# S4D convolution and feed-forward block on one core: the first part's tasks in another order, and evictions shared out anew

## The chip, the cores and the metric

One core of a Trainium2 chip runs the whole program. The metric is the device time of one execution in microseconds; the time before is the median of three runs. A profile of one execution gives every instruction's start and length on the five engines: PE (matmuls; PEld is its weight load), DVE (VectorE), ACT (ScalarE), POOL (GpSimd) and SP, which issues the DMAs.

## The reference

Sequence length 2048, width 640, state size 128, inner width 1728, all float32. `A` is the state-space convolution, `B` the feed-forward part:

```python
def A(u, ...):                      # S4D, by a transform of length 4096
    dt = exp(log_dt)
    A = -exp(log_A_real) + 1j * A_imag
    C = (C_real + 1j * C_imag) * dt[:, None]
    P = exp((A * dt[:, None])[:, :, None] * arange(L))
    K = 2.0 * einsum("dn,dnl->dl", C, P).real
    y = irfft(rfft(u_t, 2 * L) * rfft(K, 2 * L))[:, :, :L]
    return y + u * D_skip

def B(x, w1, w3, w2):
    return (silu(x @ w1) * (x @ w3)) @ w2

mod = silu(c) @ w_mod               # six rows: sa, ca, ga, sb, cb, gb
h = layernorm(x) * (1 + ca) + sa
x = x + ga * A(h)
h = layernorm(x) * (1 + cb) + sb
x = x + gb * B(h)
```

## The kernel before

The program has two parts. The first computes `x + ga * A(h)` up to the inverse transform, the second is the second layernorm and the feed-forward part, written as ordinary code; the change does not reach it.

The first part is a plan of 1507 small tasks. The width of 640 is cut into five blocks b = 0 to 4 of 128 columns, and each block goes through the same steps. A task's name says which: `g2.7` is the eighth chunk (16 columns) of block 2. The tasks that the prediction speaks of are:

- `al8b`, `expb`, `magb`: the table of exponents of block b (a product of 128x1024 by POOL or DVE, the exponentials by ACT, a product of 128x512 by POOL or DVE); `tb.h.0` to `.5` are its tables of phases.
- `gb.c.ph`, `.z0` to `.z2` (POOL, phases `ph` and sizes `xx`, `yy`), `.s0` to `.s4` (ACT, sines `tr`), `.m0` to `.m4` (DVE, products `xx`, `yy`), `.p` (PE, the chunk's kernel rows `kps`, in one half of a PSUM bank), `.r` (ACT, copied to `ks`).
- `hb.i.l`, `.n`, `.x`, `.a`, `.o`: a quarter of the block's normalised input is loaded (`xq`; for block 0 into `sp`), normalised (`hn`, four instructions on DVE or ACT), multiplied, added to (`hb`, DVE), and stored to DRAM (`hs`); `hb.f` fetches it back transposed (`xb`).
- `hhb.i.m` and `kb.i.m`: the first transform of the input and of the kernel (PE, `ps<-wk,xb` and `ps<-wk,ks`), with the evictions `.e` to `sp`, which are a COPY on DVE or an ACTIVATE on ACT.
- `wb.i.f` and `.k`: the second transform (PE, `fh` and `fk`), `.h` the eviction of `fh` to `hq` (ACT), `.x0`, `.x1`, `.c` the complex product (DVE `fp`, `fk`; POOL for w4.2 and w4.5), and `zb.j.z` the first step back (PE, `fz`), with evictions `.v0`, `.v1` to `zt` on DVE or ACT and stores to `zd` in DRAM.
- `hscale` and `fold` (DVE): the scale of the normalisation from the statistics of `xs`, and the rows of `mod` folded in. `fs0` (POOL, `wl`, `w2l`) splits feed-forward weights ahead of time.

What sets the order is the string `ORDER` (from L35 on), a list of all tasks by number, written out. `Plan.run` goes through it, and where a task may run on two engines the letter behind the number (a ACT, d DVE, p POOL) chooses one. The wrapper `InOrder` (L147) chains each instruction to the one written before it on the same engine, so that every engine, SP's DMA issues included, works through its tasks in the order of the list and waits in place for whatever is not ready:

```python
for x in ORDER.split():
    n, (engs, f, after) = T[int(x.rstrip("adp"))]
    ...
        f(dict(a="ACT", d="DVE", p="POOL")[x[-1]] if len(engs) > 1 else engs[0])
```

All instructions of the first part therefore show the wrapper's line, L147, in the profile. Fetches from DRAM are paced: such a DMA waits for the PE instruction written last before it. The product `.p` takes the halves of its bank in turn, in the order in which the products stand in the list.

Of the kernel before, what the change touches and what calls it, by code (L numbers as in the profile page):

```python
# [34 lines left out]
1 2 8 7 12 78 80 3 79 86 81 41 14 19 82 20 42 84 21 15 83 43 85 16 153p 44 17 4 22 154 18 23 28 61 45 59 30 120 31 46 121 24  # L35
10 29 25 39 156 35 26 13 62 157 60 158 47 72 74 70 76 66 89 27 48 5 93 87 91 98 49 36 100 33 95 50 94 34 51 32 88 37 52 38
155p 40 92 159d 53 96 160 90 9 161 6 54 102 162 170 104 55 173 99 11 174 171 97 56 103 186 179 175 57 105 181 176 172 58 190
187 111 180 107 188 67 195 101 122 189 68 191 177 196 163 197 192 64 182 178 123 193 183 109 164 166d 65 184 194 202 113 313
114 115 110 199 185 112 298 117 203 335 206 118 204 124 303 138 308 140 167 198 211 116 212 108 106 168 205 165 142 127 207
336a 208 209 213 119 214 130 131 210 218 63 128 132 139 129 134 215 141 216 143 200 69 419p 71 222 223 133 135 169 422 425p  # L40
423 219 221 234 220 426 235 237 236 125 136 304d 229 420 224 309a 310 305 227 144 75 73 77 126 311 228 217 314a 201 225 226
306 146 339 427 421p 250 424 230 231 315 232 251 252 253 312 299a 238 307 300 316 244 301 317 302 243 239 245 340a 240 233 241
242 254 246 255 256 337 145 247 259 248 147 341 257 261 260 258 338d 148d 262 266 270 267 268 269 282 318 149 150 263 275 151
271 249 272 342a 264 273 265 277 276 343 428 278 152 283 285 284 274 345 286 279 327 280 333 329 436 0 564 569 344a 287 288
289 291 346d 293 292 294 328a 290 281 440 334a 441 330a 442 437 439 438 452 570d 445 295 571 447 572 446 319 565a 137 579 566
443 448 320a 456 444 325 296 457 321 322a 331 453 454 567 326d 461 462 347 332d 449 458 297 323 349 348a 459 324a 460 568 829
573 580d 351 450 357 350d 581 429 684p 685 430 455 468 484 432p 469 470 471 582 830d 353 352 463 831 464 465 832 354 834 583
574 358 835a 472 575a 836 355 356 837 477 576 1359 577 466 368 359 408 370 473 474 369 409 475 1360a 451 360 479 361 478 362
371 480 476 488 467 489 487 433 434 431 686p 485 486 435 500 687 949p 578 839 833 584 481 1361 494 372 493 373 495 1362 374
391 482 490 491 392 492 840a 375 503 516 501 502 1109 838 585 1363 586 1099 376 1110a 504 385 497 496 841 377 498 842 378 1111  # L50
379 509 1112 510 843 587 380 402 505 511 506 507 483 386 499 508 520 383a 512 513 514 598 521 381a 403 522 599a 523 515 590
591a 517 518 519 532 1100d 526 525 1101 527 1102 588 536 524 528 589d 384 844 1113 363 602 537 845a 364a 535 533 688 534 548
689 529 543 366d 541 530 387 551 549 846 542 847 388 690d 691 692 550 538 603a 539 596 540 597a 552 389 545 390 544 557 558
592 593a 600 594 1103 1364 382 365 848 1104 849 404 1365a 546 1366 850 851 1094 367 852 405 601a 595a 553 554 693 406 559 407
# [1842 lines left out]
```

## Time and profile before

| | |
|---|---|
| median of 3 runs | 945.79 us (944.59 to 947.17) |
| the profiled execution's own time | 945.84 us |
| its span | 944.0 us |
| busy in the span | PE 849.6, DVE 700.5, ACT 515.1, POOL 346.4 us |
| first matmul of the feed-forward part | 374.6 us |

The span is what the profile covers; the profiled execution's own time is 1.8 us longer. The busy shares are means over two parts that differ: in the first 374.6 us all engines work, in the rest PE works nearly alone. Waits are named by what ended them; "issue" is a wait that nothing in the profile explains.

### The profile page before, as it was taken

What the parts mean: (1) busy time and instruction counts of PE and PEld (TensorE: products, weight loads), DVE (VectorE), ACT (ScalarE), POOL (GpSimd) and SP (SyncE); (2) the same over time, 40 slices, a digit from 0 to 9 for tenths busy, and PEclk for the clock granted to TensorE, in tenths of its full rate; (3) what the DMA queues carried; (4) which work ended last, traced back from release to release, by engine and by line L of the source; (5) the groups of instructions that cost most, each with busy time, mean ns of one, the idle gap of its engine ahead of it and who ended that gap; (6) DMA issues with size and microseconds to landing.
All of it is one profiled execution on the core that took longest, in us unless ns stands there. A gap on an engine that the chain in (4) does not pass through costs nothing.

```text
span 944.0 us, 22044 instructions
## 1 busy us (share of the span) xinstructions
PE 849.6 (90%) x8963; PEld 674.2 (71%) x8963; DVE 700.5 (74%) x1232; ACT 515.1 (55%) x886; POOL 346.4 (37%) x355
## 2 busy tenths in 40 slices
PE   2176779899999887999999999999999999999997
PEld 1035768767868653777877788888888888888775
DVE  7898999999999856476666666376567777765663
ACT  5889999899888733333333244354343444454331
POOL 2799999899989552000000000001133333100000
PEclk9587989999999998999999999999999999999999
DMA  9985556133041658965525262322132211123242
GB/s 244 241 255 126 170 147 170 48 104 103 27 124 40 177 149 232 254 182 153 151 64 146 84 161 77 111 84 70 42 84 70 57 50 48 38 77 111 77 149 82
DMA packets 124941, 112.78 MB, mean 119 GB/s; under 512 B 12328, under 2 KB 107048, under 8 KB 123560
## 3 DMA queue, kind: packets, MB, share of 16 engines
q1 hardware_dynamic: 124072, 110.46, 43.0%
q8 instruction: 70, 1.15, 0.5%
q10 hardware_dynamic: 768, 0.92, 0.4%
q14 instruction: 31, 0.25, 0.1%
HBM read 90.38 MB, written 20.97 MB: 118 GB/s over the span
## 4 chain that ended last, share of the span: by engine, by line
PE 67%; DMA 10%; DVE 8%; ACT 6%; issue 3%; POOL 3%; SPq 1%; DVEq 0%; ACTq 0%; POOLq 0%
PE p L820 17%; PE acc L1067 16%; PE gu L1030 6%; PE gu L1032 6%; PE gu L1031 6%; PE ps L147 4%; PE fz L147 3%; DMA low<-zd 3%; PE kps L147 2%; PE fk L147 2%; DVE yy L147 2%; PE fh L147 2%; DVE fp L147 1%; DMA wq<-in_w 1%; ACT hn L147 1%
## 5 line engine op out<-in xcount | busy, mean ns | idle before, releaser
L1030 PE MATMUL gu<-xh,wh 128*128 128x512 f32 x270 | 106.2, 398 | 1.9 <-ACT xh L609 1.1
L1032 PE MATMUL gu<-xh,wl 128*128 128x512 f32 x270 | 105.4, 390 | 0.0
L1031 PE MATMUL gu<-xl,wh 128*128 128x512 f32 x270 | 105.2, 390 | 0.0
L147 ACT ACTIVATE tr<-ph 128x512 f32<-128x512 f32 (+1 forms) x160 | 92.9, 599 | 7.0 <-DVE yy L147 5.5
L839 POOL TENSOR_TENSOR ws<-wp 128x256 f32<-128x256 f32 x13 | 9.6, 739 | 230.9 <-DVE x L610 116.0
L147 POOL TENSOR_TENSOR ph<-p,p 128x1024 int32<-128x1024 int32 x40 | 78.2, 1955 | 3.0 <-ACT tr L147 2.7
L147 DVE TENSOR_TENSOR yy<-yy,tr 128x512 f32<-128x512 f32 (+1 forms) x80 | 75.4, 942 | 1.5 <-ACT tr L147 1.2
L723 ACT ACTIVATE wh<-wr 128x640 fp32r<-128x640 f32 x51 | 34.9, 731 | 70.5 <-PE gu L1031 55.6
L820 PE MATMUL p<-x,wch 128*128 128x512 f32 x208 | 68.3, 389 | 0.0
L1030 PEld LDWEIGHTS gu<-xh,wh 128*128 128x128 f32 x270 | 50.6, 188 | 18.3 <-issue 2.1
L147 PE MATMUL kps<-yy,xx 128*32 128x64 f32 x2560 | 49.3, 228 | 10.8 <-DVE xx L147 4.6
L1032 PEld LDWEIGHTS gu<-xh,wl 128*128 128x128 f32 x270 | 50.7, 188 | 11.2 <-DVE wl L733 0.4
L736 POOL MEMSET w2l<- 64x640 f32 x1 | 0.6, 631 | 157.8 <-PE acc L1067 157.8
L1031 PEld LDWEIGHTS gu<-xl,wh 128*128 128x128 f32 x270 | 50.7, 188 | 10.2 <-DVE xl L610 0.2
L147 DVE TENSOR_TENSOR xx<-tr,xx 128x512 f32<-128x512 f32 x80 | 54.3, 680 | 1.1 <-ACT tr L147 0.8
L857 DVE TENSOR_TENSOR s<-p,s 128x512 f32<-128x512 f32 x52 | 34.7, 682 | 27.0 <-ACT s L855 23.0
L147 POOL TENSOR_TENSOR yy<-e,e 128x512 f32<-128x512 f32 x48 | 52.7, 1109 | 4.5 <-PE kps L147 2.5
L147 PEld LDWEIGHTS kps<-yy,xx 128*32 128x32 f32 x2560 | 43.2, 113 | 11.6 <-POOL yy L147 4.5
L1045 DVE TENSOR_TENSOR a<-a,gu 128x512 f32<-128x512 f32 x26 | 17.8, 686 | 45.0 <-PE gu L1032 44.9
L1043 ACT ACTIVATE th<-gu 128x512 f32<-128x512 f32 x26 | 15.5, 596 | 64.3 <-PE gu L1032 64.3
L147 PE MATMUL ps<-wk,xb 128*64 128x128 f32 x640 | 47.1, 296 | 3.0 <-ACT sp L147 1.4
L147 PE MATMUL fh<-sp,wb 128*64 128x128 f32 x640 | 44.4, 284 | 4.9 <-DVE fp L147 2.2
(377 smaller groups left out, 2380.8 us busy)
## 6 DMA issues: line engine op xcount, KB each, us to landing
wr<-in_w SPq DMA_DIRECT2D x52, 320.0 KB, 3.7
zd<-zt SPq DMA_DIRECT2D x39, 256.0 KB, 2.7
w2r<-in_w SPq DMA_DIRECT2D x26, 320.0 KB, 3.1
wp<-in_w SPq DMA_DIRECT2D x26, 320.0 KB, 3.6
wq<-in_w SPq DMA_DIRECT2D x26, 320.0 KB, 3.2
low<-zd SPq DMA_DIRECT2D x48, 160.0 KB, 5.8
xs<-in_x SPq DMA_DIRECT2D x16, 320.0 KB, 10.3
hs<-hb SPq DMA_DIRECT2D x20, 256.0 KB, 2.4
```

Of the source, the lines that this page charges most:

```text
L147: self.prev = self.k.order(f(*a, **kw), self.prev)
L723: self.nc.scalar.activation(wh[:, i], raw[:, i], AF.Copy)
L736: self.nc.gpsimd.memset(w2l[64:].bitcast(F32), 0.0)
L820: nc.tensor.matmul(to, t[:, o], y[:, k], start=start and k == i == 0, stop=stop and (k, i) == (n - 1, 2), skip_group_check=True)
L839: G.tensor_tensor(s[0], a21, a22, op=ALU.add)
L857: add = lambda o, bk, s: V.tensor_tensor(o, bk, s, op=ALU.add)
L1030: nc.tensor.matmul(pg, wh[:, k, :], xh[:, k, :], start=(k == 0), stop=False)
L1031: nc.tensor.matmul(pg, wh[:, k, :], xl[:, k, :], start=False, stop=False)
L1032: nc.tensor.matmul(pg, wl[:, k, :], xh[:, k, :], start=False, stop=(k == KT - 1))
L1043: nc.scalar.activation(th, gu[0], AF.Tanh, scale=0.5)
L1045: nc.vector.tensor_mul(a, a, gu[1])
L1067: nc.tensor.matmul(acc[k], *two(a, w), start=(m == 0 and i == 0), stop=(m == 12 and i == 2))
```

## The change

Only the string `ORDER` differs. It has the same 1507 numbers in another order, and for some tasks another letter. It is one line shorter, so that the wrapper's line is L146 afterwards. The first line of it stands for the rest:

```diff
 ORDER = """
 
-1 2 8 7 12 78 80 3 79 86 81 41 14 19 82 20 42 84 21 15 83 43 85 16 153p 44 17 4 22 154 18 23 28 61 45 59 30 120 31 46 121 24
+1 2 3 4 78 79 5 80 6 81 20 14 82 19 7 41 84 8 21 83 15 11 42 153d 9 43 154 22 44 23 16 24 17 25 18 45 30 59 26 28 27 96 91 87 29
 ...
 """
```

Engines: 25 evictions go from DVE to ACT and 17 from ACT to DVE; of the normalisations `.n` four go to ACT and three to DVE; al80, al81, mag0, mag1 and four table steps go from POOL to DVE, two table steps from DVE to POOL.

At the start, SP issued `w_mod` (into `sp`) and two tables ahead of the loads of x (`xs`), here from the last parameter load on:

```order
L147 DMA x_e<-in_a_im 128x5x128
L147 DMA sp<-in_w_mod 128x1920 x2
L147 DMA wk<-in_t_wk 128x256
L147 DMA wz<-in_t_wz 128x256
L147 DMA xs_164<-in_x 32x2560 x2
L147 DMA xs_164<-in_x 32x4x640 x2
L147 DMA xs_194<-in_x 32x2560 x2
L147 DMA xs_194<-in_x 32x4x640 x2
L147 DMA sp<-in_w_mod 128x1920
```

Now all four loads of x stand directly behind the parameters:

```order
L146 DMA x_e<-in_a_im 128x5x128
L146 DMA xs_142<-in_x 32x2560 x2
L146 DMA xs_142<-in_x 32x4x640 x2
L146 DMA xs_147<-in_x 32x2560 x2
L146 DMA xs_147<-in_x 32x4x640 x2
L146 DMA xs_170<-in_x 32x2560 x2
L146 DMA xs_170<-in_x 32x4x640 x2
L146 DMA xs_176<-in_x 32x2560 x2
L146 DMA xs_176<-in_x 32x4x640 x2
L146 DMA sp<-in_w_mod 128x1920 x2
```

The loads of x moved ahead of all of `w_mod`; the two tables follow later. POOL's first products before (the row with `al` is al80, that with `mag` mag0, the first `ph` is the phase of chunk g0.0):

```order
L147 TENSOR_TENSOR ks_133<-al,j_109 128x1024
L147 TENSOR_TENSOR x_e<-x_e,pB 128x128
L147 TENSOR_TENSOR p_118<-p_118,step 128x128x2
L147 TENSOR_TENSOR p_118<-p_118,step 128x128x4
L147 TENSOR_TENSOR x_e<-x_e,pB 128x512
L147 TENSOR_TENSOR pB<-pB,x_e 128x128
L147 TENSOR_TENSOR e_122<-e_122,mag 128x128x4
L147 TENSOR_TENSOR p_119<-p_119 128x128
L147 TENSOR_TENSOR p_119<-p_119,step 128x128x2
L147 TENSOR_TENSOR ph_312<-p_118,p_119 128x1024
```

And now:

```order
L146 TENSOR_TENSOR x_e<-x_e,pB 128x128
L146 TENSOR_TENSOR p_118<-p_118,step 128x128x2
L146 TENSOR_TENSOR pB<-pB,x_e 128x128
L146 TENSOR_TENSOR p_118<-p_118,step 128x128x4
L146 TENSOR_TENSOR x_e<-x_e,pB 128x512
L146 TENSOR_TENSOR p_119<-p_119 128x128
L146 TENSOR_TENSOR p_119<-p_119,step 128x128x2
L146 TENSOR_TENSOR ph_298<-p_118,p_119 128x1024
```

The two products with `al` and `mag` are gone from POOL's list; DVE has them. On PE the place that matters is the product of chunk g2.7 (`kps` from `yy_368`; `yy_352` is chunk g2.6; `fh26` is w2.6's, `fk17` w1.7's). Before:

```order
L147 MATMUL fk17_3107<-sp_85,wb_84 64x128 x8
L147 MATMUL kps_391<-dsk_74,ident_58 32x4 x4
L147 MATMUL kps_391<-yy_352_3001,xx_352_3000 32x64 x32
L147 MATMUL fh26_3160<-sp_85,wb_84 64x128 x8
L147 MATMUL fh27_3169<-sp_85,wb_84 64x128 x8
L147 MATMUL fh25_3178<-sp_85,wb_84 64x128 x8
...
L147 MATMUL ps306_3257<-wk_72,xb_86 64x4x16x2 x8
L147 MATMUL ps304_3266<-wk_72,xb_86 64x4x16x2 x8
L147 MATMUL kps_391<-dsk_74,ident_58 32x4 x4
L147 MATMUL kps_391<-yy_368_3007,xx_368_3006 32x64 x32
```

The "..." stands for k2.0's 32 rows. Now the same place reads:

```order
L146 MATMUL kps_427<-yy_352_2766,xx_352_2765 32x64 x32
L146 MATMUL fz110_3037<-fp12_2741,wz_73 128x512
L146 MATMUL fz111_3038<-fp12_2741,wz_73 128x512
...
L146 MATMUL fk14_3053<-sp_85,wb_84 64x128 x8
L146 MATMUL fk16_3074<-sp_85,wb_84 64x128 x8
L146 MATMUL kps_427<-dsk_74,ident_58 32x4 x4
L146 MATMUL kps_427<-yy_368_2857,xx_368_2856 32x64 x32
L146 MATMUL fh21_3132<-sp_85,wb_84 64x128 x8
L146 MATMUL fh23_3144<-sp_85,wb_84 64x128 x8
L146 MATMUL fk15_3160<-sp_85,wb_84 64x128 x8
L146 MATMUL fk17_3172<-sp_85,wb_84 64x128 x8
```

The product of g2.7 moved up past the `fh` of block 2, k2.0 and two input transforms of block 3 (`ps306`, `ps304`), which now come behind it. Near the end of the first part w4.0's and w4.1's `fk` come ahead of w4.2's, six evictions of block 4 go to ACT, and `fs0`, which POOL did between two steps of w4.2, is last. The products `gb.c.p` now run in the order of their numbers (g0.0, g0.1, g0.2 ...), where before some pairs were swapped (g0.0, g0.2, g0.1 ...), so that a chunk's rows may lie in the other half of their bank.

More of the change, by code (lines that the diff above doesn't have):

```diff
@@ L39 @@
[L39 to L54, printed above, removed]
@@ new lines @@
+562 712 707 1369 389 639 695 623 711 708 718 1106 650 721 713 640 720 563 850 393 709 1103 1107 719 365 722 714 1108 633 651
+697d 727 733 723 667 390 547 724 728 616 668 726 949p 725 394 715 737 730 634 729 617 698 851 610 734 738 395 731 736 612d 396
+950 673 735 742 611d 749 852 1095d 607 696 739 608d 1096 656 752 674 743 1097 699 744 604 740 750 700 609d 741 745 865 751 606a
+605a 746 853 716 765 753 866d 754 759 747 854a 760 755 952 758 414 657 1370d 769 756 867 766 415a 761 417a 757 768 613 418 1371
@@ new lines @@
+1073 1163 1221 926 1082 1079 1147 1074 1152 1164 1081 919 910 1083 1080 1075 1084 920 1222 1153 1087 934 1045 1219 1089 1085
+913a 1088 940 911a 935 1223 1231 1086 912 1076 936 941 927 1091 1235 1247 1090 1061 937 928a 1482 1092 1248 914 1236 942 929
+930a 1140 943 1232 1237 1137 1216d 1077 1093 1141a 1142d 1234 1238 1380 1197 1139a 1233 1242 1186 1138d 1239 1250 1241 1134 1187
+1240 1249 1198 1251 1243 1381 944 1224 1136a 1135d 1252 1244 1253 1143 1257 945a 1263 1258 1245 947a 1144d 1145a 1256 1254 1382
@@ new lines @@
+1165 1267 1264 1259 1255 1203 1266 1260 1268 1148 1166 1269 1279 1167 1169 1246 1149 1204 1274 1483 1180 1225 1283 948 1168
+1227p 1261 1181 1150 1265 1270 1272 1170 1391 1228 1273 1282 1271 1275 1395 1280 1151 1284 1397 1281 1396a 1276 1285 1290 1171
+1226 1288 1286 1393 1289 1229 1287 1291 1392a 1277 1230 1295 1172 1154 1398d 1173 1389 1299 1296 1174 1300 1297 1155 1394a 1487
+1387 931 1301 1390d 946 1311 1292 1383 1262 1278 1156 1293 1305 1384a 1298 1302 1304 1175 1294 1307 1312 1315 1388a 1157 1314
@@ new lines @@
+1316 1306 1176a 1488 1158 1313 1178a 1320 1177 1303 1179 1322 1317 1327 1321 1199 1308 1161a 1318 1205 1200 1319 1323 1182 1343
+1159a 1201 1331 1484 1385 1206 1160 1183 1309 1386a 1207 1332 1202 1188 1328 1324 1208 1330 1489 1325 1347 1184 1336 1470 1344
+1189 1435 1471 1185 1345 1333 1338 1428 1346 1353 1436 1190 1310 1492 1209 1329 1348 1162 1191 1349 1337 1429 1352 1411 1334
+1210d 1212a 1485 1402 1335 1211 1412 1340 1404a 1493 1192 1354 1350 1339 1403a 1326 1399 1195a 1351 1196 1341 1356 1193a 1401a
@@ L88 @@
+1355 1194 1405 1213 1357 1406a 1417 1358 1407a 1400a 1464 1418 1342 1497 1481 1408 1452 1410a 1409a 1490 1486 1413 1419 1414
+1453 1420 1498 1465 1430 1421 1437 1415 1431 1432 1416 1446 1422 1433 1438 1499 1423 1439 1434 1440 1426a 1494 1454 1447 1448
+1455 1424a 1449 1500 1441 1450 1456 1425 1427 1495 1457 1466 1442d 1451 1502 1467 1458 1472 1443 1468 1444a 1473 1496 1445 1459
+1469 1474 1475 1460a 1503 1476 1462a 1461 1463 1491 1501 1477a 1479a 1478 1480 1504 1505 1506
 """
```

67 lines of the change are left out of this document (31 added, 36 removed).

## The prediction

> **What bounds the kernel now.** I read first the busy time of each engine, cut into five stretches at points of the program (the end of the input statistics, the last vector product of chunk g2.7, the last spectrum product on TensorE, the first matmul of the feed-forward part), then what the engines wait for in the second and third of them. The columns of the windows are time, length, then busy microseconds and instruction counts of PE, PEld, DVE, ACT and POOL, granted clock, DMA share and rate.
>
> ```profile
> core 0: us, PE busy (x) PEld busy (x) DVE busy (x) ACT busy (x) POOL busy (x), PEclk, DMA share, GB/s
> 0.00:67.50 67.50, 24.29 (x253) 12.06 (x257) 57.87 (x123) 47.31 (x99) 43.11 (x61) 0.77 0.93 242
> 67.50:228.40 160.90, 133.40 (x3096) 110.89 (x3088) 154.96 (x264) 149.74 (x269) 150.77 (x146) 0.94 0.49 133
> 228.40:335.10 106.70, 100.17 (x2748) 81.67 (x2750) 96.42 (x159) 85.13 (x155) 85.64 (x80) 1.00 0.32 86
> 335.10:374.60 39.50, 31.50 (x239) 17.20 (x233) 26.17 (x76) 11.81 (x20) 15.91 (x14) 0.91 0.76 206
> 374.60:944.00 569.40, 560.22 (x2638) 452.41 (x2638) 365.11 (x614) 221.15 (x347) 51.01 (x57) 1.00 0.37 102
> ```
>
> The feed-forward part, 569.4 us, is PE almost alone (560.2 busy), and its code and order are the same in both kernels, so only the first 374.6 us can change. There the bound changes hands. From 67.5 to 228.4 DVE is busy 154.96 of 160.90 us (96%) while PE has 27.5 us without work; from 228.4 to 335.1 PE is busy 100.17 of 106.70 (94%). The hand-over is one place in the order, the product g2.7.p:
>
> ```profile
> 225.90 0.68 DVE L147 TENSOR_TENSOR xx<-tr,xx 128x512 f32<-128x512 f32 x1
> 226.50 1.20 DVE L147 TENSOR_TENSOR yy<-yy,tr 128x1024 f32<-128x1024 f32 x1
> 228.45 1.16 PE L147 MATMUL kps<-yy,xx 128*32 128x64 f32 x64 [1.01 <-DVE xx L147]
> 335.16 0.69 DVE L147 TENSOR_TENSOR fp<-fk,hq 128x512 f32<-128x512 f32 x1 [2.97 <-PE fk L147]
> ```
>
> The third row is g2.7.p, which PE began after waiting 1.01 us for DVE; behind it PE hardly stops until, in the fourth row, DVE itself has waited 2.97 us for the last `fk`. So the end of the first part is reached by one path: DVE's list up to g2.7.p, then PE's list behind it, then the tail. What each of the two engines still waited for in its stretch (columns: total, times, longest; first DVE 67.5 to 228.4, then PE 228.4 to 335.1):
>
> ```profile
> DVE sp L147 <- PE ps L147: 1.7, 3, 1.0
> DVE hn L147 <- ACT hn L147: 1.4, 1, 1.4
> DVE yy L147 <- ACT tr L147: 1.2, 3, 0.7
> DVE hn L147 <- ACT zt L147: 0.3, 1, 0.3
> ...
> PE ps L147 <- issue: 3.1, 3, 1.4
> PE kps L147 <- issue: 2.2, 2, 1.6
> PE fk L147 <- issue: 0.6, 1, 0.6
> ```
>
> DVE waits 4.6 us in all, PE 5.9 us for nothing that the profile names.
>
> **The change, part by part.** No task is added or removed. Time can only come from where a task stands relative to g2.7.p, and from which of two engines does it.
>
> (1) DVE's list ahead of g2.7.p. By the two orders, 31 tasks of DVE that stood ahead of it now stand behind it or are done by ACT or POOL, and 19 come in. Their rows (mean ns in the last column but one; window 67.5 to 335.1):
>
> ```profile
> L147 DVE TENSOR_TENSOR yy<-yy,tr 128x1024 f32<-128x1024 f32 x37 | 44.8, 1210 | 1.5 <-ACT tr L147 1.2
> L147 DVE TENSOR_TENSOR fp<-fp,fk 128x256 f32<-128x256 f32 x64 | 23.7, 410 | 0.1
> L147 DVE TENSOR_TENSOR fk<-fk,hq 128x512 f32<-128x512 f32 x32 | 22.1, 692 | 0.0
> L147 DVE TENSOR_TENSOR fp<-fk,hq 128x512 f32<-128x512 f32 x32 | 21.7, 680 | 0.7 <-PE fk L147 0.6
> L147 DVE COPY sp<-ps 128x512 f32<-128x512 f32 x27 | 18.0, 682 | 7.0 <-PE ps L147 7.0
> L147 DVE TENSOR_SCALAR hn<-xq,rs_y_h,rs_n_h 128x128 f32<-128x128 f32 x24 | 9.8, 412 | 1.0 <-ACT zt L147 0.3
> L147 DVE TENSOR_TENSOR e<-e,mag 128x512 f32<-128x512 f32 x1 | 1.5, 1489 | 0.0
> L147 DVE TENSOR_SCALAR p<-pB 128x128 int32<-128x128 int32 x2 | 1.3, 660 | 0.0
> ```
>
> Out: four normalisations of four instructions, 16 x 0.412 = 6.6; thirteen evictions by `COPY`, 13 x 0.682 = 8.9; the products of w1.4 to w1.7, 4 x (0.680 + 0.692 + 2 x 0.410) = 8.8; mag4 1.5; one table step 0.7: together 26.4 us in 47 instructions. In: al80 and al81, costed as the 128x1024 row, 2 x 1.21 = 2.4; mag0 and mag1, 2 x 1.49 = 3.0; three normalisations 4.9; nine evictions 6.1; three table steps 2.0: 18.5 us in 28 instructions. Net -7.9 us. Two neighbours overlap a little (225.90 + 0.68 ends 0.08 after 226.50 begins), so 19 instructions fewer give back 19 x 0.08 = 1.5: **-6.4 us**. Over the whole first part DVE's work is the same to within 0.2 us by the same rows; what leaves comes back behind g2.7.p, where PE's list covers it as long as PE is the longer one.
>
> (2) DVE's start. Its early waits, and operations that took far longer than their size:
>
> ```profile
> 9.65 2.04 DVE L147 TENSOR_TENSOR xb<-x_e 128x128 f32<-128x128 f32 x1
> 30.27 0.17 DVE L147 TENSOR_SCALAR st_n<-st_n 128x4 f32<-128x4 f32 x1 [0.57 <-ACT xs L147]
> 36.40 1.51 DVE L147 TENSOR_SCALAR st_n<-st_n 128x4 f32<-128x4 f32 x1 [1.24 <-ACT xs L147]
> 40.93 0.69 DVE L147 SCALAR_TENSOR_TENSOR yy<-yy,tr 128x512 f32<-128x512 f32 x1 [0.96 <-POOL yy L147]
> 27.11 0.29 DVE L147 TENSOR_TENSOR xb<-x_e 128x128 f32<-128x128 f32 x1
> ...
> 9.12 2.42 POOL L147 TENSOR_TENSOR ks<-al,j 128x1024 f32<-128x1024 f32 x1 [6.88 <-ACT al L147]
> 32.18 1.48 POOL L147 TENSOR_TENSOR e<-e,mag 128x512 f32<-128x512 f32 x1
> 35.94 1.95 POOL L147 TENSOR_TENSOR ph<-p,p 128x1024 int32<-128x1024 int32 x1
> ```
>
> The 128x128 operation at 9.65 took 2.04 us beside POOL's al80 at 9.12, and an operation of the same form took 0.29 at 27.11: 1.75 us lost, and al80 is no longer on POOL. The two waits for `xs` (0.57 and 1.24) should go, since the four loads of x are now issued ahead of those of `w_mod`; the 0.96 us for POOL's `yy` too, since al80 and mag0 (the row at 32.18) no longer stand ahead of the first phases. Together **-4.6 us**. Bounds: nothing, if these waits change their place, and about 6, if also the 1.51 us of the four-column operation at 36.40 goes. The same amount of `w_mod` is loaded ahead of the scale as before, so I add nothing for the later place of these loads; what it could cost is a rival below.
>
> (3) DVE's waits up to g2.7.p. PE's list ahead of that point becomes 14 us lighter (below), so I drop the 1.7 us that DVE waited for `ps` and leave the other three: **-1.7 us**. Bounds: -4.6 (all) and +4.6 (as much again, should the later input stores and transform fetches of block 0 be felt).
>
> (4) PE's list behind g2.7.p. Thirteen tasks that stood ahead of it now stand behind it: seven `fh` (w2.0, 1, 3 to 7), two `fk` (w1.5, w1.7), two `ps<-wk,xb` (hh3.4, hh3.6), one `ps<-wk,ks` (k2.0), one `fz` (z1.2). None goes the other way. The rows of that stretch:
>
> ```profile
> L147 PE MATMUL kps<-yy,xx 128*32 128x64 f32 x1088 | 20.1, 221 | 3.2 <-issue 2.2 <-DVE xx L147 1.0
> L147 PE MATMUL fk<-sp,wb 128*64 128x128 f32 x292 | 19.9, 278 | 0.6 <-issue 0.6
> L147 PE MATMUL fz<-fp,wz 64*128 64x512 f32 x72 | 18.7, 614 | 0.0
> L147 PE MATMUL fh<-sp,wb 128*64 128x128 f32 x240 | 16.5, 281 | 0.1
> L147 PE MATMUL ps<-wk,xb 128*64 128x128 f32 x224 | 16.5, 296 | 0.0
> L147 PE MATMUL ps<-wk,ks 64*64 64x64 f32 x704 | 13.6, 222 | 3.6 <-issue 3.1 <-ACT ks L147 0.5
> L147 PE MATMUL kps<-dsk,ident 128*32 128x4 f32 x128 | 3.9, 183 | 0.0
> ```
>
> A task has 16 matmuls (`fz` 8, `ps<-wk,ks` 64): `fh` 16.5 x 16/240 = 1.10, `fk` 1.09, `ps<-wk,xb` 1.18, `ps<-wk,ks` 1.24, `fz` 2.08. So 7 x 1.10 + 2 x 1.09 + 2 x 1.18 + 1.24 + 2.08 = 15.6. Matmuls overlap: the seven rows add to 109.2 where the engine was busy 100.17, so 15.6 x 0.917 = 14.3. The one thing that leaves this stretch is w4.2's `fk`, now behind w4.0's instead of ahead: -1.0. **+13.3 us.** Bounds: 13.3, if the path is as I read it, and 13.3 - 5.9 = 7.4, if the moved tasks fill PE's 5.9 us of waits there.
>
> (5) The edits with nothing on the path. ACT takes over more evictions than it gives (net 6.7 us), and was busy 85 of 107 us in the third stretch; POOL loses 7 us and no row of DVE's waits from 67.5 on names POOL; the six evictions of block 4 that go to ACT are covered by PE's list. The weight split that POOL did between two steps of w4.2 now comes last on POOL; the tail behind 335.1 waits for DVE's products, `fz` and the stores and loads of `zd`, which keep their order, so I take 0. The halves of the chunk bank change turn at the same price.
>
> Sum: -6.4 - 4.6 - 1.7 + 13.3 = +0.6. The profiled execution took 945.84 us (its span ends at 944.0, the end of the last window), the median of the three runs is 945.79, so nothing is corrected for: **946.4 us**, no change that can be measured, which for this kernel means within 0.3%, or 2.8 us (943.0 to 948.6).
>
> **Rivals.**
> - *PE has room behind the hand-over* (faster). The thirteen tasks fill PE's 5.9 us of waits there; for it: these waits are for nothing the profile names, and other tasks now stand at those places. Against: fetches from DRAM come just as late, in the same alternation. 946.4 - 5.9 = 940.5. It decides once over 3.4 us of the waits are filled.
> - *The start's gain does not come* (slower). DVE's in-order list meets its waits elsewhere, for the row broadcast that hangs on `w_mod`, now behind the loads of x. For it: DMA is 93% busy in the first stretch, so what is loaded sooner makes something else later. Against: the bytes ahead of the fold are the same. 946.4 + 4.6 = 951.0. It decides once 2.2 of the 4.6 us stay.
> - *POOL's load holds up DVE everywhere* (faster). Then al81 and mag1, which leave POOL, free DVE of their time as well in the full stretch: by the two rows of POOL above, 1.95 + 1.48 = 3.4, so 943.0. For it the row at 9.65; against it that in the second stretch both engines are busy over 93%, and that the 128x512 products there take 0.68 us, as the row at 225.90 shows.
> - *The change is hidden* (DVE stays the bound to the end): only the start counts, 945.8 - 4.6 = 941.2, which I count with the first. Against: behind 228.4 DVE has 10 us to spare, and the last row of the second fence shows it waiting for PE.
>
> The Trainium skill, SBUF — State Buffer, section "SBUF: two separate sides", says that a DVE operation with two SBUF inputs and a GpSimd operation that reads SBUF hold a shared pair of ports as an exclusive lock, and the other fully blocks. It is the third rival's rule: the operation at 9.65 agrees (2.04 us where 0.29 is usual), the filled stretch does not (0.68 us a product with POOL 94% busy), so I go by the rows. By the rule the sum would be 943.0.
>
> **How the numbers follow.** Chances: the forecast 0.34 (its own range 943.0 to 948.6), the first and fourth rival 0.25, the lock 0.07 (on the line, half to each side), the second rival 0.25, and 0.09 for stalls beyond it. Faster by over 0.3%: 0.25 + 0.04 = 0.29; within: 0.34 + 0.03 = 0.37; slower: 0.25 + 0.09 = 0.34. The range takes in both rivals and the bounds of (3): from 940.5 - 2.9 = 937.6 to 951.0 + 4.6 = 955.6.
>
> **What would show it.** Right: DVE's last product of g2.7 ends near 228.3 - 12.7 = 215.6 and the last `fk` of w4.0 near 335.7; the 128x128 operation beside al80 takes 0.3 us; the scale of the normalisation ends some 5 us sooner; from there to the feed-forward part 39.5 us, as now. Wrong: PE idle for more than 7 us behind g2.7.p, or DVE waiting over 5 us between 62 and 215 us for a fetch or the broadcast; or a first matmul of the feed-forward part that does not move with w4.0's `fk`.

## The result, and the profile after

The changed kernel took 959.22 us (median of 4 runs, 957.07 to 960.55) against 946.48 for the kernel before: a ratio of 1.0131, 95% interval 1.0099 to 1.0164. It is 12.7 us slower. A second series beside other runs gave 958.44 us (1.0113, interval 1.0095 to 1.0131). The profiled execution's span is 956.1 us, 12.1 more than before.

The five stretches of the first view, cut at the same points of the program in the new kernel (the end of `hscale`, DVE's last product of g2.7, the last `fk` of w4.0, the first matmul of the feed-forward part; columns as before):

```profile
core 0: us, PE busy (x) PEld busy (x) DVE busy (x) ACT busy (x) POOL busy (x), PEclk, DMA share, GB/s
0.00:63.00 63.00, 19.71 (x215) 9.98 (x219) 54.40 (x121) 43.50 (x89) 31.93 (x47) 0.97 0.92 245
63.00:220.50 157.50, 126.84 (x2878) 102.14 (x2870) 148.34 (x246) 145.03 (x268) 145.19 (x143) 0.93 0.45 127
220.50:346.50 126.00, 113.91 (x2992) 93.04 (x2990) 103.95 (x174) 97.40 (x177) 95.62 (x90) 1.00 0.33 89
346.50:387.40 40.90, 33.81 (x254) 17.05 (x250) 25.41 (x75) 12.46 (x22) 16.13 (x14) 0.83 0.75 210
387.40:956.10 568.70, 560.00 (x2638) 452.45 (x2638) 365.11 (x614) 221.56 (x347) 51.05 (x57) 1.00 0.36 101
```

| | before | after | difference | predicted | after, second profile |
|---|---|---|---|---|---|
| start to `hscale` | 67.5 | 63.0 | -4.5 | -4.6 | 63.4 |
| `hscale` to g2.7 | 160.9 | 157.5 | -3.4 | -8.1 | 154.8 |
| g2.7 to w4.0's `fk` | 106.7 | 126.0 | +19.3 | +13.3 | 126.5 |
| tail | 39.5 | 40.9 | +1.4 | 0 | 41.6 |
| feed-forward part | 569.4 | 568.7 | -0.7 | 0 | 571.1 |

The last column is a second profile of the changed kernel, taken beside the runs below (span 957.4 us). Between the two, single stretches differ by up to 2.7 us, so a difference of that size in one stretch of one profile says little.

The hand-over (DVE's last product of g2.7, its `yy`, and with it g2.7.p on PE) did come earlier, at 220.5 instead of 228.4 us, though not at 215.6:

```profile
218.71 0.68 DVE L146 TENSOR_TENSOR xx<-tr,xx 128x512 f32<-128x512 f32 x1
219.31 1.21 DVE L146 TENSOR_TENSOR yy<-yy,tr 128x1024 f32<-128x1024 f32 x1
220.69 1.15 PE L146 MATMUL kps<-yy,xx 128*32 128x64 f32 x64
```

PE came to g2.7.p straight from an `fk` and began it without a wait, where it waited 1.01 us for DVE before. At this place the two lists are now level, so a DVE list shortened further by itself would hardly have brought g2.7.p forward; no run tests that.

Most of the loss lies behind it: 19.3 us where 13.3 were forecast. PE is busy 113.9 there instead of 100.2 us (+13.7: the thirteen tasks), and idle 12.1 instead of 6.5. What PE waited for in that stretch of the new kernel (total, times, longest):

```profile
PE kps L146 <- issue: 3.4, 2, 2.0
PE ps L146 <- issue: 2.8, 3, 1.0
PE fk L146 <- DVE fp L146: 1.5, 3, 0.8
PE ps L146 <- ACT zt L146: 1.2, 1, 1.2
PE ps L146 <- DVE fp L146: 0.6, 1, 0.6
PE fk L146 <- ACT zt L146: 0.6, 1, 0.6
```

The waits that nothing explains are as large as before (6.2 and 5.9 us). New are those for DVE's products and ACT's evictions, most of which empty a PSUM bank that PE is to fill next. With the smaller rows, PE's waits for DVE and ACT there are 5.5 us, and 5.2 in the second profile; before they were 1.5, of which 1.0 is g2.7.p itself. The plainest difference between the two kernels is the chain of work that ended last, taken for this stretch alone, first before (230 to 335 us), then after (222 to 346 us), by share of the chain:

```profile
by line: PE ps L147 27.2%; PE kps L147 18.3%; PE fz L147 17.4%; PE fk L147 16.5%; PE fh L147 14.8%; issue 5.7%; ACT ks L147 0.4%
```

```profile
by line: PE ps L146 15.1%; issue 10.5%; PE fz L146 9.6%; PE kps L146 8.9%; DVE fp L146 7.8%; PE fh L146 7.3%; DVE yy L146 6.3%; PE fk L146 5.6%; DVE fk L146 5.0%; DMA zd<-zt 3.8%; POOL ph L146 3.1%; POOL p L146 3.0%; DVE xx L146 2.9%; ACT s
```

Before, PE makes up 94% of it. After, PE's five entries add to 46.5% and DVE's four to 22%; the rest is POOL, ACT, stores and issue. Behind the hand-over the work now passes from engine to engine and no longer follows one list.

The other shortfall is between `hscale` and g2.7. DVE is busy 148.34 of 157.50 us there, so it waits or pauses 9.2 us where it did 5.9 (7.5 in the second profile):

```profile
DVE sp L146 <- PE ps L146: 4.7, 4, 3.4
DVE yy L146 <- ACT tr L146: 1.6, 2, 1.3
DVE hn L146 <- ACT hn L146: 0.8, 1, 0.8
DVE hn L146 <- DMA xq<-in_x: 0.8, 1, 0.8
```

One wait of 3.4 us stands out. It ends at 108.3 us. The second profile does not have it: `sp` waits 1.0 us for PE there, and `hn` 2.6 us for ACT in its place. In windows of 20 us, before and then after, DVE, ACT and POOL all lose time around it:

```profile
80.00:100.00 20.00, 17.41 (x434) 14.82 (x435) 19.38 (x34) 18.82 (x36) 20.00 (x17) 0.92 0.72 195
100.00:120.00 20.00, 15.53 (x372) 13.84 (x374) 19.71 (x36) 19.29 (x34) 18.41 (x20) 0.93 0.43 123
```

```profile
80.00:100.00 20.00, 13.84 (x336) 11.00 (x332) 17.77 (x31) 15.38 (x31) 18.94 (x21) 0.93 0.57 157
100.00:120.00 20.00, 15.84 (x282) 14.43 (x286) 16.24 (x26) 16.74 (x32) 13.56 (x13) 0.74 0.75 212
```

DVE is busy 34.0 of these 40 us instead of 39.1, ACT 32.1 instead of 38.1. The timeline of PE in the new kernel shows where it comes from:

```profile
100.93 1.98 PE L146 MATMUL ps<-wk,ks 128*64 128x128 f32 x16 [4.24 <-ACT ks L146]
104.56 5.39 PE L146 MATMUL ps<-wk,xb 128*64 128x128 f32 x48 [1.65 <-DMA xq<-in_x]
```

PE first waits 4.24 us for a chunk's rows, then for block 0's input, which is fetched when the last quarter h0.3 is stored. (The row names the load `xq`, but what came in then was the last part of that fetch, issued at 99.1 and landed 5.3 us later, at 104.4.) The matmuls behind these waits are slow: three input transforms take 5.39 us, where one takes 1.18 by the row of the full stretch; the window's granted clock is 0.74.

### The profile page after: what moved, and what is told of

Same layout as the page of the kernel before. It is cut to its first block, busy times and chain, and to the rows that moved or that the text cites. A ratio compares the mean times of both kernels' runs of the same rounds, so it can differ in the third digit from the quotient of the medians.

```text
span 956.1 us, 21982 instructions
## 1 busy us (share of the span) xinstructions
PE 854.3 (89%) x8963; PEld 674.7 (71%) x8963; DVE 697.2 (73%) x1226; ACT 519.9 (54%) x898; POOL 339.9 (36%) x349
## 4 chain that ended last, share of the span: by engine, by line
PE 66%; DVE 13%; ACT 8%; DMA 7%; issue 4%; POOL 1%; SPq 1%; DVEq 0%; ACTq 0%; POOLq 0%
PE p L819 17%; PE acc L1066 16%; PE gu L1029 7%; PE gu L1031 6%; PE gu L1030 6%; DVE yy L146 3%; PE ps L146 3%; DMA xs<-in_x 3%; PE fz L146 2%; ACT tr L146 2%; DVE fp L146 2%; DMA wq<-in_w 2%; PE kps L146 2%; DVE xx L146 1%; ACT hn L146 1%
## 5 line engine op out<-in xcount | busy, mean ns | idle before, releaser
L146 ACT ACTIVATE tr<-ph 128x512 f32<-128x512 int32 (+1 forms) x160 | 93.4, 604 | 9.5 <-DVE yy L146 4.3
L146 POOL TENSOR_TENSOR ph<-p,p 128x1024 int32<-128x1024 int32 x40 | 79.2, 1982 | 9.8 <-ACT tr L146 9.3
L146 DVE TENSOR_TENSOR yy<-yy,tr 128x512 f32<-128x512 f32 (+1 forms) x80 | 75.5, 944 | 4.2 <-ACT tr L146 1.9
L146 PE MATMUL kps<-yy,xx 128*32 128x64 f32 x2560 | 47.8, 224 | 11.3 <-DVE xx L146 4.1
L146 DVE TENSOR_TENSOR xx<-tr,xx 128x512 f32<-128x512 f32 x80 | 54.0, 681 | 3.6 <-ACT tr L146 3.5
L146 POOL TENSOR_TENSOR yy<-e,e 128x512 f32<-128x512 f32 x48 | 52.7, 1103 | 8.9 <-PE kps L146 5.3
L146 PE MATMUL ps<-wk,xb 128*64 128x128 f32 x640 | 50.0, 306 | 6.4 <-DVE fp L146 1.8
L146 PEld LDWEIGHTS ps<-wk,xb 128*64 128x64 f32 x640 | 45.0, 220 | 13.9 <-ACT tr L146 3.0
L146 PEld LDWEIGHTS kps<-yy,xx 128*32 128x32 f32 x2560 | 42.1, 111 | 12.0 <-issue 4.7
```

Source lines behind the costliest of these rows:

```text
L146: self.prev = self.k.order(f(*a, **kw), self.prev)
```

## The experiments

All are timed against the kernel before on the same chip (947 us). A list in a diff names tasks in the order in which they are written.

**The new start alone**

```diff
 ORDER:
+ the new order and engines, from the first task to hscale
  all tasks left, in the order and on the engines of before
```

> The new order up to the scale of the normalisation (hscale) with its new engines, then everything else in the order of before. Theory of the lists (the first part ends when DVE's list up to g2.7.p, then PE's list behind it, are done): DVE keeps the 4.5 us by which hscale ends sooner in the new kernel, PE's list behind g2.7.p is that of before: 946.5 - 4.5 = 942.0. Rival, that an early gain is given back to the first fetch or broadcast that comes at its old time: 946.5, with DVE waits of 4 us or more between 63 and 224 us.

950.38 us, ratio 1.003 (1.001 to 1.005). Both expectations fail. `hscale` ended 2.7 us sooner, but g0.2's five products (3.9 us) still lay behind it, and the chunk after that, g0.3, was done at 83.2 us instead of 79.7. Two waits of DVE were longer than before, when the first took 1.4 us and the second did not show:

```profile
DVE hn L150 <- ACT hn L150: 2.7, 1, 2.7
...
DVE rw L150 <- ACT wb L150: 1.0, 1, 1.0
```

An early `hscale` is no gain in itself: the new start does al80, al81 and mag0 on DVE in place of g0.2's products. Up to the end of g0.3's products, where both have done the same chunks (before, then the new start alone):

```profile
0.00:79.70 79.70, 28.18 (x353) 15.21 (x353) 67.85 (x138) 59.21 (x120) 55.31 (x71) 0.76 0.86 229
```

```profile
0.00:83.20 83.20, 30.69 (x353) 15.76 (x353) 69.52 (x141) 59.28 (x120) 52.00 (x68) 0.85 0.80 220
```

DVE is busy 1.7 us more, with three instructions more, and idle 13.7 instead of 11.9 us: 3.5 us later in all, and the whole run is 2.9 us longer. So the start gives nothing by itself, and less than nothing where the tasks behind it are not arranged for it.

**The two parts of the new order apart**

```diff
 e2 ORDER:
  the order and engines of before, up to the product g3.0.p
+ all tasks left, in the new order and on the new engines
 e3 ORDER:
+ the new order and engines, up to the product g3.0.p
  all tasks left, in the order and on the engines of before
```

> The order of before up to the product g3.0.p, then all that is left in the new order with its engines; the thirteen PE tasks and the DVE tasks that the change moves behind g2.7.p are done ahead of it as before. Theory of the lists: the 13 to 15 us on PE are gone, and so is DVE's extra load behind that point; only the tail's 1.4 us can stay: 946.5 to 948. Rival, that the new order behind that point has waits of its own (PE waited 5.6 us more there in the new kernel, for DVE's fp and ACT's zt): 952 to 954.

> The new order up to g3.0.p with its engines, then all that is left in the order of before. Theory of the lists: DVE hands over about 8.9 us sooner, PE's list behind it is about 14 us longer, and PE waits for DVE's later products: 946.5 - 8.9 + 14 to 20 = 952 to 958. Rival, that the loss sits in the order behind the hand-over: 946.5 or less.

951.03 us (1.0037, 1.0016 to 1.0058) and 953.58 us (1.0058, 1.0037 to 1.0079). The first falls between its two expectations, the second is where the lists put it. Both halves of the new order cost time, 3.5 and 6.1 us. Together that is 9.6 of the 12.7; no run shows where the other 3.1 come from, and each half also brings a join of its own between the old order and the new. In the second one w4.0's last `fk` ended 8.3 us later than before, from a hand-over 7.1 us earlier.

**The thirteen PE tasks alone**

```diff
 ORDER:
- w2.0.f w2.1.f ... w1.5.k w2.3.f w2.4.f z1.2.z w1.7.k ... w2.6.f w2.7.f w2.5.f k2.0.m hh3.6.m hh3.4.m ... g2.7.p
+ ... g2.7.p w2.0.f w2.1.f ... w1.5.k w2.3.f w2.4.f z1.2.z w1.7.k ... w2.6.f w2.7.f w2.5.f k2.0.m hh3.6.m hh3.4.m ...
```

> The order of before, with the thirteen PE tasks (seven fh of block 2, w1.5's and w1.7's fk, z1.2's fz, k2.0, hh3.4, hh3.6) and the tasks that need their results (nine of them on DVE: two complex products, three evictions) moved from ahead of g2.7.p to right behind it; no engine changes. Theory of the lists: DVE's list up to g2.7.p loses 6.4 us, PE's list behind it gains 14.3: 946.5 + 7.9 = 954.4, or up to 960 with new waits of PE for those products. Rival, that PE's room hides the move: 941 to 948.

961.13 us, ratio 1.0135 (1.0093 to 1.0177), 13.6 us slower. That work moved behind g2.7.p is not hidden is confirmed; the size is again larger than the lists say. DVE's list up to g2.7.p lost 6.4 us, but DVE got there only 2.8 us sooner: its idle time on the way rose from 5.9 to 8.7 us, in waits for ACT, POOL and PE. PE ran dry:

```profile
218.12 1.96 PE L150 MATMUL kps<-yy,xx 128*32 128x64 f32 x64 [4.61 <-POOL p L150]
...
225.66 1.96 PE L150 MATMUL kps<-yy,xx 128*32 128x64 f32 x64 [5.52 <-DVE xx L150]
227.55 3.59 PE L150 MATMUL fh<-sp,wb 128*64 128x128 f32 x32
```

```profile
215.00:225.00 10.00, 2.02 (x72) 1.96 (x72) 7.49 (x13) 9.63 (x14) 9.60 (x14) 0.61 0.41 114
225.00:235.00 10.00, 9.23 (x150) 8.46 (x152) 3.85 (x7) 4.00 (x6) 6.63 (x6) 0.70 0.01 2
```

In ten microseconds PE works 2.0, while ACT and POOL are full (9.6 each); in the next ten DVE and ACT work 4. And a product that takes 1.16 us takes 1.96 after the pause, at a granted clock of 0.61 to 0.70. As one lump, the move costs both sides of the hand-over.

**The engines alone, and the order alone**

```diff
 e4b ORDER: order of before
-... each task on the engine of before
+... each task on its new engine (59 tasks change)
 e4 ORDER: new order
-... each task on its new engine
+... each task on the engine of before
```

> The order of before word for word, each task on the engine that the change gives it (DVE +0.2 us over the first part, ACT +6.7, POOL -7.0). Theory (the order moves the hand-over and makes the loss; the engines alone matter only at the start): al80, al81, mag0 and mag1 on DVE add about 5 us ahead of the hand-over, the 1.75 us beside al80 go, and of the evictions nine leave and seven come: 946.5 + 1 to 5 = 947.5 to 951. Rival, that the shared-out evictions carry the loss: 955 or more.

> The new order with every task on the engine that it had before. Theory that order and engines are fitted to one another, so that either half of the change alone is worse than both (the engines alone cost 31 us): 965 to 985. Theory that the new engines are the loss, whatever the order: 947 or less.

977.85 us (1.0333, 1.0311 to 1.0355) and 974.4 us (1.0275, 1.0248 to 1.0302). Either half of the change alone costs more than twice what both cost together. My theory for the engines missed by 27 us: it counted work (DVE +0.2 us), not places. With the engines alone, DVE waits six times for a normalisation that ACT now does at a point of the order where DVE wants it at once:

```profile
DVE hn L150 <- ACT hn L150: 12.7, 6, 5.1
```

**The wait at 108 us**

```diff
 ORDER (new):
- ... h0.3.n h0.1.o ... h0.3.x ... h0.3.a h0.3.o ... h1.1.l h1.3.l h0.f
+ h0.3.n ... h0.1.o h0.3.x h0.3.a h0.3.o h0.f ... h1.1.l h1.3.l
```

> The new kernel, with the normalisation of the last input quarter of block 0 (h0.3), its store and the fetch of the block pulled up to right behind h0.1's, some 6 us sooner in DVE's list; nothing else. Theory that part of the missed gain up to the hand-over is the one wait of 3.4 us of DVE for PE's ps, behind that fetch: it goes, and 959.2 - 3 = 956. Rival, that the hand-over is held by ACT's and POOL's lists as well, so that the wait only moves: 959.

960.43 us, ratio 1.0141 (1.0114 to 1.0169): nothing gained. The fetch went out at 91.0 instead of 96.4 us, and PE still waited 3.40 us for `ks` ahead of it and began the input transforms at 105.7 instead of 104.6. DVE's longest wait for `ps` fell from 3.4 to 2.2 us, and others came for it (0.9, 0.8 and 0.8 us for PE and POOL). The rival is right: behind the fetch PE's wait had a second reason of the same length. As a second profile of the unedited kernel has no such wait of DVE either, this run says little on what that one wait cost.

**The loads of x alone**

```diff
 ORDER (before):
- T ... x0 ... x1 ... x2 ... x3
+ T x0 x1 x2 x3 ...
```

> The order of before, with SP's four loads of x pulled up to right behind the parameters, as the change has it; nothing else. The prediction's start term: DVE's two waits for xs (1.8 us) go, and 946.5 - 1.8 = 944.7. Rival, that what is loaded later (w_mod) takes it back at the broadcast and the fold: 946.5 to 950.

958.75 us, ratio 1.0125 (1.0101 to 1.0149): 11.9 us slower, beyond the rival too. PE's list still has the matmuls on `w_mod` (`pm`) ahead of transposes that DVE needs, and `w_mod` now comes later:

```profile
PE pm L150 <- DMA sp<-in_w_mod: 20.2, 1, 20.2
```

```profile
DVE pB L150 <- PE ptp L150: 10.5, 1, 10.5
```

The change moves those matmuls as well, which is why it does not pay this; the prediction had costed the loads without saying so.

**al80 alone**

```diff
 ORDER (before):
- al80 on POOL
+ al80 on DVE
```

> The kernel before with al80 alone on DVE. The prediction's term for it: the operation of 2.04 us beside it takes 0.3 again, and DVE has 1.2 us more to do: 946.9 - 0.5 = 946.4, no change. Rival, that any edit of the start throws the lists out of step: 949 or more.

946.41 us, ratio 0.9982 (0.9964 to 1.0000): as expected, no change to speak of. The slow operation is quick again:

```profile
9.15 0.28 DVE L150 TENSOR_TENSOR xb<-x_e 128x128 f32<-128x128 f32 x1
```

In the changed kernel this gain is lost again a little later. POOL, without al80 and mag0, begins its first phases sooner (32.91 instead of 35.94 us), and they now meet a product of DVE that takes 2.32 us, where others of its form take 0.68:

```profile
32.91 4.63 POOL L146 TENSOR_TENSOR ph<-p,p 128x1024 int32<-128x1024 int32 x2
33.41 2.32 DVE L146 TENSOR_TENSOR xb<-x_e 128x512 f32<-128x512 f32 x1
```

The run with the new start alone has it too (2.32 us).

**Which list sets the end behind the hand-over**

Two kernels leave out work behind g2.7.p without touching the order: half of the `fz` matmuls of blocks 2 and 3 (PE, 8 us by the rows), or the second of the two last products of their sixteen w tasks (DVE, 6.6 us by the rows). In the profiles the busy time of that stretch fell by less: PE's by 4.9 us in the new kernel and 5.6 in the one before (an `fz` task of eight matmuls takes 1.99 us, one of four 1.13), DVE's by 5.3 and 4.4. Each was made from the new kernel and from the one before.

```diff
 e11, e13:  inverse(j)
-            for r in range(2):
+            for r in range(1 if b in (2, 3) else 2):
 e12, e14:  both(i, e)
-            for r, op in enumerate((ALU.subtract, ALU.add)):
+            for r, op in enumerate((ALU.subtract, ALU.add)[:1 if b in (2, 3) else 2]):
 e17: both edits, new kernel
```

> The new kernel with half of the matmuls left out in the eight fz tasks of blocks 2 and 3, all behind g2.7.p: PE's list there is 8 us shorter, DVE's is unchanged. Theory of the lists (behind the hand-over PE's list alone sets the end): 959.2 - 8 = 951. Theory of even engines (DVE's and ACT's lists are nearly as long there, so PE would wait for them instead): 954 to 957.

> The new kernel with one of the two last products left out in the sixteen w tasks of blocks 2 and 3, all behind g2.7.p: DVE's list there is 16 x 0.41 = 6.6 us shorter, PE's is unchanged. Theory of the lists: nothing but PE's 2.5 us of waits for fp goes, 956.5 to 959. Theory of even engines: about as much as PE's 8 us brings, 954 to 957.

> The kernel before with the same half of the fz matmuls of blocks 2 and 3 left out (8 us of PE's list behind g2.7.p). If PE's list sets the end there, as the prediction read it: 946.8 - 8 = 939. If DVE's list (96.4 of 106.7 us busy there) takes over: 941 to 944.

> The kernel before with the same sixteen products left out (6.6 us of DVE's list behind g2.7.p). If PE's list sets the end there: 946.8, no change. If the engines are even: 942 to 945.

> The new kernel with both things left out at once: half of the fz matmuls (8 us of PE behind g2.7.p) and sixteen of the last products (6.6 us of DVE). If the two lists are even there and each hides the other, both together give more than the two alone add up to (2.8 and 5.6 by the medians): 949 or less. If DVE alone sets the end: 953 to 954, as without PE's part.

> The new kernel once more, unchanged, as the base for the run beside it on the same chip: 959.2, within 2.

| left out | new kernel (959.22, again 958.44) | kernel before (947.02 here) |
|---|---|---|
| PE | 956.42, 1.0101 (1.0069 to 1.0132) | 943.58, 0.9972 (0.9955 to 0.9989) |
| DVE | 953.62, 1.0075 (1.0046 to 1.0104) | 945.03, 0.9982 (0.9965 to 0.9999) |
| both | 953.67, 1.0072 (1.0050 to 1.0095) | |

In neither kernel does PE's list alone set the end. Before, leaving out PE work brings 3.4 us and DVE work 2.0, though the chain runs over PE throughout. In the new kernel PE's brings 2.0 to 2.8, by intervals that overlap with those of the full kernel, and DVE's 4.8 to 5.6. Both at once bring no more than DVE's alone.

The stretch from the hand-over to w4.0's last `fk` shows how much of that arises there. In the new kernel it takes 126.0 and 126.5 us in two profiles. With PE work left out, DVE work, and both:

```profile
219.60:343.40 123.80, 108.98 (x2957) 90.86 (x2957) 103.65 (x173) 97.13 (x176) 95.58 (x90) 0.99 0.33 91
218.60:342.20 123.60, 114.30 (x2988) 94.58 (x2988) 98.66 (x157) 97.12 (x176) 95.65 (x90) 0.99 0.33 91
220.60:344.40 123.80, 110.05 (x2958) 92.27 (x2958) 99.43 (x157) 96.56 (x177) 95.91 (x90) 0.97 0.33 90
```

And before, where it took 106.7, without the PE work and without the DVE work:

```profile
226.80:331.30 104.50, 94.54 (x2716) 78.81 (x2718) 96.00 (x159) 85.10 (x156) 85.66 (x80) 1.00 0.32 87
226.60:332.00 105.40, 100.73 (x2748) 82.71 (x2750) 92.00 (x143) 84.83 (x156) 85.70 (x80) 0.98 0.33 87
```

In the new kernel each cut, and both together, shorten the stretch by the same 2.4 us or so (2.2 to 2.9): some 5 us off one list bring half of it, and 4 off each of the two bring no more (one profile each). By these profiles a third limit lies just below, which neither list makes. The rest of DVE's 4.8 to 5.6 us falls in stretches that the edit does not touch, and the hand-over of the unedited kernel itself differs by 2.3 us between two profiles; the runs do not show what this rest is. Nor is the length of DVE's list separated from its delay: the product that is left out also stands between an `fk` and the `fz` after it, so that this chain gets shorter too. The chain of the kernel with both left out (225 to 344 us) shows who comes next:

```profile
by line: PE ps L146 12.6%; PE fh L146 10.8%; PE kps L146 10.5%; issue 10.2%; POOL yy L146 7.0%; ACT tr L146 6.1%; DMA zd<-zt 5.9%; POOL ph L146 4.8%; PE fk L146 3.6%; PE fz L146 3.2%; POOL p L146 3.2%; ACT ph L146 2.9%; ACT hq L146 2.8%; AC
```

DVE's entries are gone from its head; POOL, ACT and the stores of `zt` have moved up. That these are the third limit is a reading of the chain, and not tested.

**DVE's evictions to ACT, and ACT's own list**

```diff
 e9 ORDER (new): the ten evictions of DVE between g2.7.p and w4.0.k
- z1.2.v1 k2.3.e0 k2.1.e0 ... z3.3.v0 on DVE
+ z1.2.v1 k2.3.e0 k2.1.e0 ... z3.3.v0 on ACT
 e16:  hold(i), new kernel
-            nc.scalar.activation(held[i], bank.pop((0, i)), AF.Copy)
+            n = 1 if b >= 2 else 2
+            nc.scalar.activation(held[i][:, :n], bank.pop((0, i))[:, :n], AF.Copy)
```

> The new kernel, with the ten evictions that DVE does between g2.7.p and the last fk of w4.0 given to ACT (6 us of DVE's list there); nothing else. Theory that PE's new waits behind the hand-over (for DVE's fp 2.5 us, for ACT's zt 2.0) come from DVE's list being 8.6 us longer there: they shrink, and 959.2 - 2 to 4 = 955 to 957. Rival, that PE waits for the order itself, or that ACT becomes late instead: 959 or more.

> The new kernel with half of each eviction of fh to hq left out in blocks 2 to 4 (23 behind g2.7.p, each 0.21 us shorter by the rows of 128x512 and 128x256: 5 us of ACT's list). If ACT's list is on the path behind the hand-over like DVE's (6.6 us of DVE gave 5.6): 955 to 956. If ACT has room: 958 to 959.

961.33 us (1.0161, 1.0136 to 1.0186) and 958.25 us (1.0110, 1.0082 to 1.0139). Six microseconds taken from DVE bring nothing when ACT gets them. DVE then waits for ACT's sines:

```profile
DVE yy L150 <- ACT tr L150: 5.0, 5, 2.2
DVE xx L150 <- ACT tr L150: 4.7, 4, 1.9
```

In the new kernel these two waits are 0.3 and 2.1 us. Five microseconds less on ACT by themselves bring nothing that can be told. So ACT's list by itself is no bound there; by the waits, it has no room at the places where the evictions fall.

**The moved tasks put back**

```diff
 ORDER (new):
- g2.7.m3 ... g2.7.p ... (34 tasks: w2.x.f, w1.5-7.k, w1.4-7.x0 x1 c, z1.2.z, their evictions) ...
+ (the 34 tasks) g2.7.m3 ... g2.7.p ...
```

> The new kernel, with 34 tasks pulled from behind to ahead of the last two DVE products of g2.7: the seven fh of block 2, w1.5's, w1.6's and w1.7's fk, z1.2's fz, the products of w1.4 to w1.7 on DVE (8.8 us), four evictions by DVE or ACT, and the tasks on ACT that follow them. So ten of the thirteen PE tasks and most of DVE's 8.6 us stand ahead of g2.7.p again. If the two lists behind the hand-over are the cause and where a task stands decides it: 959.2 - 6 to 10 = 949 to 953. If the new order is as full everywhere, so that one place put right moves the bound to the next one: 956 to 960.

972.82 us, ratio 1.026 (1.0238 to 1.0282): 13.6 us slower than the new kernel, outside both expectations. The largest waits are one of DVE for a store of `zt` and one of PE for DVE:

```profile
DVE zt L150 <- DMA zd<-zt: 7.3, 1, 7.3
```

```profile
PE kps L150 <- DVE yy L150: 5.6, 1, 5.6
```

Both hang on how the edit was made. It pulled the tasks ahead of a fetch of block 3's input and of stores of `zd` that stood among them. A paced fetch waits for the PE instruction written last before it, and that is now a later one, so it went out about 10 us later, and the stores behind it on SP's queue too (first the new kernel, then this run):

```profile
220.72 0.30 SPq L146 DMA_DIRECT2D xb<-hs  x1
221.14 0.92 SPq L146 DMA_DIRECT2D zd<-zt  x2
```

```profile
231.11 0.30 SPq L150 DMA_DIRECT2D xb<-hs  x1
231.50 0.93 SPq L150 DMA_DIRECT2D zd<-zt  x2
234.90 0.69 DVE L150 COPY zt<-fz 128x512 f32<-128x512 f32 x1 [7.30 <-DMA zd<-zt]
```

So this run does not price the tasks' place by itself: a good part of its loss comes with the later fetch and stores. It shows that a task can't be put back without the DMAs that were written around it.

## Why the prediction was wrong, point by point

- **What bounds the kernel** (wrong, and the root of it). The prediction read the first part as DVE's list up to g2.7.p and PE's behind it, each with the others covered. The busy shares that carried this, 96% and 94%, were true, but 90% of DVE in the second stretch, and 93% of ACT and 94% of POOL in the first, stood in the same rows. Leaving out work of PE, 5.6 us of its busy time, brought 3.4 us before, and leaving out 4.4 us of DVE's brought 2.0 (interval 0.1 to 3.3), although DVE was to be covered there. The chain of waits named PE alone, and still a second chain lay a few microseconds under it. (The cut at 335.1, called the last spectrum product, is w4.0's `fk`; six more `fk` of block 4 follow in the tail.)
- **(1) DVE's list ahead of g2.7.p**: -6.4. DVE's busy time up to the hand-over fell from 212.8 to 202.7 us, by 10.1: the 8.2 of (1) and of the blocked operation, and 1.9 more. The list as such was counted rightly.
- **(2) The start**: -4.6, measured -4.5 at `hscale`. The four terms add to 4.5, and the agreement is luck. With the new list, `hscale` ended at 62.8 to 65.6 us in ten profiles, and it comes sooner since g0.2's five products (3.9 us) now stand behind it and al80, al81 and mag0 ahead of it. DVE's idle time in the start fell by 1.0 us only (from 9.6 to 8.6): the waits for `xs` (1.8 to 0.4) and POOL's `yy` (1.3 to none) went, but 1.4 more for ACT's `tr` and 0.6 for a parameter load came. Of the 1.75 us of the blocked operation, 1.6 were lost again by the product at 33.41. And alone, the new start costs 2.9 us.
- **(3) DVE's waits**: -1.7 was taken; they grew by 3.2 us (9.2 against 5.9; by 1.6 in the second profile). The term is off by 4.9, as much as the hand-over lacks, 220.5 against 215.6. A lighter PE list did not make PE punctual: around block 0's fetch DVE, ACT and POOL all lose time, and an earlier fetch did not remove that.
- **(4) PE's list**: +13.3 was forecast, PE's busy time rose by 13.7. Right.
- **(5) The edits costed at nothing** (the term that failed by most). DVE's list behind the hand-over grew from 96.4 to 104.0 us, ACT's from 85.1 to 97.4, and the prediction let PE's list cover both. Instead PE waited for DVE's products and ACT's evictions, its idle time there rose from 6.5 to 12.1 us (10.1 in the second profile), and the stretch took 6.0 us more than forecast. That is the sign of being wrong that the prediction named, PE idle for more than 7 us behind g2.7.p. Leaving out some 5 us of PE's work, of DVE's or of both takes the same 2.4 us or so off, so PE's list alone does not set the end.
- **The tail**: 0 was taken, +1.4 measured (+2.1 in the second profile). w4.2's `fk` (1.0 us) was taken out of the stretch ahead and added nowhere, though it now stands in the tail. The run with only the later part new has a longer tail too: from w4.0's `fk` to the last `fz` 18.4 us, in the new kernel 18.5, before 17.3; the runs that keep the old end have 17.3 to 17.7. The evictions of block 4 that go to ACT are eight, not six (six of k4 and two of z4).
- **The sum**. The span was to grow by 0.6 us and grew by 12.1. The 11.5 us between are 0.1 of the start, 4.7 up to g2.7, 6.0 behind it and 1.4 of the tail, less 0.7 of the feed-forward part.
- **The rivals**. The faster ones are out. The second rival, a start whose gain does not come, fits the run of the start alone in kind: the four terms brought little, and DVE's waits came up elsewhere. The result is beyond it, and the range was too narrow because each term's bounds were taken from one list at a time.

The third rival rested on DVE and POOL holding each other up. The Trainium skill, SBUF — State Buffer, section "SBUF: two separate sides", says that a DVE operation with two SBUF inputs and a GpSimd operation that reads SBUF exclude each other. The traces agree with it where they have such a pair: 2.04 us beside al80 (0.28 without), and 2.32 beside POOL's phases. The prediction's test in the full stretch was misread: the products of 0.68 us there take `tr`, `fk` or `hn` from PSUM and have only one input in SBUF, so the row at 225.90 says nothing for or against. The rival is out by other numbers: al81 and mag1 left POOL, these products still take 0.68 us, and the kernel became slower. al80 alone on DVE brings 1.1 us by the medians, with an interval from nothing to 3.4.

What stays open: which of the joints behind the hand-over makes how much of the 6.0 us, and what the third limit is. Both lists shortened together still leave the new kernel 6.5 us behind the old one, and no single edit of its order or engines that was tried brought it nearer. No order was found that beats the kernel before by more than the measurement can tell.

## What to carry to other kernels

Where every engine goes through a fixed list and three of them are over 90% busy at once, a sum over the longest list does not give the time of a change. What is taken from one list can come back as a wait of the next (here some 5 us of busy time left out brought 2 to 3 in its stretch), and a list that is called covered comes onto the path when a few microseconds are added to it. Order and engine choice are one fit; half of such a change can cost more than the whole, so neither a gain nor a loss can be read from a part of it. Before calling work covered, leave some of it out and see what comes back: two runs of that kind would have shown that PE was not the only bound. And an edit that is to test one thing has to carry along the DMAs that are written around the tasks it moves.

## What the runs showed of the hardware

PE's granted clock falls with its pauses inside a kernel: after waits of 4.61 and 5.52 us, `kps` products took 1.96 instead of 1.16 us, at 0.61 and 0.70 in their windows, and three input transforms after waits of 4.24 and 1.65 us took 5.39 instead of some 3.5. Shorter pauses close together do it too: in the run of the new start alone, behind waits of 1.30, 1.45 and 1.74 us, `kps` took 1.95 instead of 1.16 us. The Trainium skill, TensorE: Matmul & The Clock Gate, "What's actually happening", describes such a throttle that returns after an idle window of about 3.4 us; the trace agrees with it in that the pauses above that length are followed by slow matmuls. So a late input can be paid twice, by the wait and by the slow matmuls after it, and a lump of work moved off PE's list can cost more than its length.

A DVE product with both inputs in SBUF was held up beside a POOL operation (128x128: 2.04 us beside al80, 0.28 without; 128x512: 2.32 beside the phases), while 128x512 products with one input in PSUM kept 0.68 us with POOL 94% busy.
